# Agent attention and two feed-forward layers: nine query blocks' probabilities turned by VectorE and transfers while the layers run, query scores as two column tiles, and a new order of the opening

## The chip, the cores and the metric

The program runs on one core of a Trainium2 chip. The metric is the device time in microseconds (us) of one execution; the number that counts is the median over executions. A core has TensorE (PE; its weight loads are listed as PEld), VectorE (DVE), ScalarE (ACT), GpSimd (POOL) and SyncE (SP), which here issues nearly all transfers. Inputs and output lie in HBM; the engines work on SBUF and PSUM.

## The reference

```python
# q, k, v: [1, 12480, 128]; agents: [1, 49, 128]; all float32
a2k = softmax(scale * agents @ k.T)          # [49, 12480]
agent_v = a2k @ v                            # [49, 128]
q2a = softmax(scale * q @ agents.T)          # [12480, 49]
x = q2a @ agent_v                            # [12480, 128]
h = x @ w_in;   x = (h * sigmoid(h)) @ w_out # w_in [128, 2048], w_out [2048, 128], float64
h = x @ w2_in;  out = (h * cos(h)) @ w2_out  # the second layer, of the same sizes
```

## The kernel before

**Opening.** The 12480 tokens are cut into 13 blocks S: twelve of 1024 tokens (128 partitions by 8) and one of 192. For each block of k: `kT` turns it on PE (8 transposes), `kX` copies the turned block out of PSUM on ACT, `kS` makes the 49 agents' scores on PE, `kM` keeps them and their maximum on DVE. After the last k block the maximum is known (`x0` to `x4`); then `vE` (ACT), `vt` (PE), `vc` (ACT), `va` (PE) sum the probabilities times v. For each block of q: `qT` and `qX` turn it, `qS` makes the scores (PE, line 379), `qM`, `qB`, `qE`, `qZ`, `qR` make the softmax on DVE and ACT, `qN` scales it on POOL. Then `qP`, `qK`, `qL` on POOL pack high part, low part and a part of the high one again into 128 rows, `qt` turns the pack on PE in two halves of 4 transposes (line 440), and `qk` copies each half out of PSUM into the tile `pT` on ACT (line 445). `pT` is what the first layer multiplies, token by token; `qt` and `qk` of all 13 blocks stand in the opening or among the first groups.

The weights come as float64 in 16 pieces, each split by integer and float operations into a high and a low float32 part: `dA` and `dH` on ACT, `d0` to `d4` and `dL` on DVE. At the end of the opening `c0` to `c6`, `cA`, `cP`, `cl`, `cH`, `cs` and `cw` multiply the attention's sums into the first layer's weights, so that the first layer reads probabilities in place of x. Of 98 rows the product's high and low parts fit 128 partitions but for 19, which a second, small product adds (line 689) from the tile `x`, loaded out of `pT` by four transfers.

**Order.** Every engine works through its own instructions in the order in which they are written. Three hand-written tables set it: `ORDER` (the opening), `FIRST` (the first layer's groups 0 to 4 with what is left of the opening) and `LOADS` (the transfers of weight pieces w, and blocks k, q, v). A load waits until a buffer is free: 5 for k and q together, 3 for w, 3 for v. SP issues them in the table's order.

**Layers.** Tokens go in 25 tiles t of 512 (the last three are shorter); each tile has four groups, so there are 100 groups g. From group 5 on a loop body does the first layer's group g and, beside it, the second layer's group q = g - 5: per group 40 matmuls of 512 columns and four small ones on PE. Of the other engines' work the prediction uses these: ACT line 789 (rounds h / 2 pi) releases DVE line 799 (the remainder), ACT line 808 (sine), DVE line 816 (times h; one operand in PSUM), DVE line 825 (cast to the high part), POOL line 834 (low part, two per group, started after DVE line 724). DVE line 724 is the first layer's low part (both operands in SBUF). PE's three pairs of PSUM banks go round: the second layer's `L2_h(q, 0)` (line 775) takes the pair that DVE line 816 of the group before has freed. `L2_end` (line 856) turns a finished tile 32 by 32 on DVE and SP stores it.

Of the kernel before, what the change touches and what calls it, by code (L numbers as in the profile page):

```python
# [39 lines left out]
kX10 qR0 dL3 qN0 dA5 kM8 kT9 qM1 qP0 qB1 kS10 qK0 qL0 qE1 qT2 kX9 qZ1 d05 qt0.0 qX2 d15 kT11 qR1 d34 qk0.0 qN1  # L40
kS9 dA6 kM10 kT12 d44 kX11 qS2 qP1 kM9 dH5 qK1 d25 qL1 qt0.1 qM2 kS11 qk0.1 qB2 kX12 qt1.0 d35 qE2 qT3 qk1.0 d06
dL4 kS12 qX3 qT4 kM11 d45 dA7 qt1.1 qS3 d16 qX4 d07 kM12 dH6 x0 qZ2 qT5 qk1.1 d17 x1 qR2 qS4 dH7 qM3 qN2 qX5 x2
qP2 qB3 qK2 x3 qT6 qE3 x4 qL2 qM4 vE12 qZ3 qS5 vE0 d26 qR3 dL5 qN3 qX6 qt2.0 qB4 qT7 d27 qE4 qP3 dA8 qZ4 vt1 qK3
qT8 qM5 qk2.0 qL3 qB5 qX7 qt2.1 qR4 d08 qS6 qN4 qk2.1 d36 vc1 qP4 qE5 vt0 vE2 qM6 qT9 qK4 qB6 qL4 qZ5 qt3.0 vc0
d46 va1 qX8 d18 vt3 qk3.0 vt2 d28 vc3 qR5 va0 d37 qN5 vc2 dL6 qE6 qt3.1 va3 qk3.1 qP5 vE4 d47 qT10 qK5 qt4.0 dA9
qZ6 vt4 qL5 dH8 d09 qS7 qk4.0 d38 vc4 dL7 vE8 qt5.0 qS8 qR6 d19 qN6 qk5.0 qM7 dA10 qB7 qt4.1 qX9 d29 vt5 d48 qP6
va2 qk4.1 qM8 qE7 qK6 qB8 va4 qL6 vE6 qZ7 qt5.1 d39 qS9 vc5 dL8 vE10 qR7 d010 qN7 vt6 qM9 qE8 va5 qB9 qP7 vc6 z0
qK7 d110 vt7 dA11 qL7 va6 qk5.1 qZ8 vc7 z1 qt6.0 qX10 z2 d210 vt9 d310 qT11 qk6.0 d011 dH9 d111 qt6.1 qE9 qS10
qR8 d49 qk6.1 qN8 qZ9 dH11 qR9 vc9 qT12 dL9 qP8 qt7.0 dH10 va7 qM10 qX11 qK8 d410 vt10 qN9 qk7.0 va9 qB10 dL10
qE10 qt7.1 qX12 qS11 dA12 qP9 qZ10 qL8 z3 vc10 d012 qk7.1 qK9 vt8 dA13 qM11 qt8.0 qL9 vc8 va10 qB11 qk8.0 d013  # L50
# [897 lines left out]
```

## Time and profile before

| | |
|---|---|
| median of 3 executions | 1080.2 us (1079.47 to 1080.25) |
| span of the profiled execution, first to last instruction | 1076.8 us |
| own time of the profiled execution | not listed apart; 1080.2 less 1076.8 leaves 3.4 us around the span |
| PE busy | 1065.2 us (99%) |
| DVE busy | 964.1 us (90%) |
| ACT busy | 909.8 us (84%) |
| POOL busy | 504.0 us (47%) |
| granted TensorE clock, mean | 0.999 |

A busy PE is not PE at its peak: matmuls overlap, their ends are modelled, and what counts is the distance from one start to the next. Idle time of an engine costs something only where another waits for it.

### The profile page before, as it was taken

The page shows a single profiled execution, that of the slowest core. Times are in us where ns is not written, and L with a number is a line of the kernel's source. Part 1 is how long each engine was busy: PE and PEld are TensorE (multiplying, and loading weights), DVE is VectorE, ACT ScalarE, POOL GpSimd, SP SyncE. Part 2 cuts the span into 40 slices and gives each one's busy share as a digit, 9 for nine tenths or more (in the row PEclk, how much of TensorE's full clock was granted, in tenths as well). Part 3 has the DMA queues.
Part 4 walks back from the last instruction along what each step waited for, and adds up shares of the span by engine and source line. Part 5 has one row for each costly group of instructions (what it writes and reads, how often), then busy time and mean ns, then how long its engine had stood idle before and what let it go on. Part 6 is the DMA issues. An engine that isn't in the chain of part 4 may idle for free.

```text
span 1076.8 us, 14174 instructions
## 1 busy us (share of the span) xinstructions
PE 1065.2 (99%) x5267; PEld 841.2 (78%) x5267; DVE 964.1 (90%) x1067; ACT 909.8 (84%) x972; POOL 504.0 (47%) x264
## 2 busy tenths in 40 slices
PE   9999999999999999999999999999999999999997
PEld 5897777777777777777777777777777777788996
DVE  7877999989999999999989998999999999999897
ACT  5888988888888888888888888888888888888876
POOL 0445044554455445544554455445544554455555
PEclk9999999999999999999999999999999999999999
DMA  9963000000000000000000000000000000000000
GB/s 345 344 226 125 9 6 11 6 16 13 4 16 16 1 17 16 1 16 17 10 6 16 12 5 16 13 4 16 17 1 16 16 1 15 15 11 5 12 9 15
DMA packets 66221, 38.68 MB, mean 36 GB/s; under 512 B 52523, under 2 KB 57184, under 8 KB 66152
## 3 DMA queue, kind: packets, MB, share of 16 engines
q1 hardware_dynamic: 65352, 37.68, 11.5%
q8 instruction: 41, 0.67, 0.3%
q14 instruction: 28, 0.23, 0.1%
q10 hardware_dynamic: 800, 0.10, 0.1%
HBM read 27.58 MB, written 6.39 MB: 32 GB/s over the span
## 4 chain that ended last, share of the span: by engine, by line
PE 95%; DVE 2%; ACT 1%; POOL 1%; DMA 1%; issue 1%; SPq 0%; POOLq 0%; DVEq 0%; ACTq 0%
PE y L733 16%; PE y L737 16%; PE y L734 16%; PE h L701 10%; PE h L775 8%; PE h L777 8%; PE h L776 8%; PE h L689 4%; PE h L267 2%; PE h L379 2%; PE h L303 1%; PE y L366 1%; PE y L440 1%; POOL g2l L834 1%; DMA kraw<-in_k_dram 1%; DVE g L816 1%
## 5 line engine op out<-in xcount | busy, mean ns | idle before, releaser
L834 POOL TENSOR_TENSOR g2l<-g,g2h 128x1024 fp32r<-128x1024 f32 (+2 forms) x200 | 465.5, 2349 | 498.7 <-DVE g1l L724 489.0
L799 DVE SCALAR_TENSOR_TENSOR n<-n,h 128x1024 f32<-128x1024 int32 (+3 forms) x202 | 239.0, 1184 | 63.9 <-ACT n L789 50.8
L789 ACT ACTIVATE n<-h,quarter 128x1024 int32<-128x1024 f32 (+3 forms) x202 | 219.8, 1088 | 88.7 <-PE h L777 88.6
L724 DVE TENSOR_TENSOR g1l<-g,g1h 128x1024 fp32r<-128x1024 f32 (+2 forms) x200 | 239.7, 1199 | 9.7 <-ACT g1h L716 4.1
L816 DVE TENSOR_TENSOR g<-n,h 128x1024 f32<-128x1024 f32 (+3 forms) x202 | 238.0, 1179 | 4.0 <-ACT n L808 0.7
L709 ACT ACTIVATE g<-h 128x1024 f32<-128x1024 f32 (+2 forms) x200 | 199.4, 997 | 36.2 <-PE h L701 36.0
L808 ACT ACTIVATE n<-n,halfpi 128x1024 f32<-128x1024 f32 (+3 forms) x202 | 225.6, 1119 | 0.8 <-DVE n L799 0.8
L716 ACT CAST g1h<-g 128x1024 fp32r<-128x1024 f32 (+2 forms) x200 | 204.9, 1025 | 3.2
L825 DVE CAST g2h<-g 128x1024 fp32r<-128x1024 f32 (+2 forms) x196 | 155.5, 794 | 7.5
L733 PE MATMUL y<-g1h,o1h 128*128 128x512 f32 (+2 forms) x400 | 156.4, 391 | 0.1
L733 PE MATMUL y<-g2h,o2h 128*128 128x512 f32 (+2 forms) x400 | 154.9, 387 | 1.1 <-DVE o L856 0.9
L775 PE MATMUL h<-x2h,i2h 128*128 128x512 f32 (+2 forms) x400 | 154.2, 386 | 1.0 <-DVE g L816 1.0
L734 PE MATMUL y<-g2h,o2l 128*128 128x512 f32 (+2 forms) x400 | 154.5, 386 | 0.0
L734 PE MATMUL y<-g1h,o1l 128*128 128x512 f32 (+2 forms) x400 | 154.0, 385 | 0.0
L777 PE MATMUL h<-x2l,i2h 128*128 128x512 f32 (+2 forms) x400 | 153.9, 385 | 0.0
L776 PE MATMUL h<-x2h,i2l 128*128 128x512 f32 (+2 forms) x400 | 153.9, 385 | 0.0
L701 PE MATMUL h<-pT,w2h 128*128 128x512 f32 (+2 forms) x400 | 132.3, 413 | 0.0
L737 PE MATMUL y<-g2l,o2h 128*128 128x512 f32 (+2 forms) x400 | 122.3, 387 | 1.9 <-POOL g2l L834 1.9
L737 PE MATMUL y<-g1l,o1h 128*128 128x512 f32 (+2 forms) x400 | 121.2, 384 | 0.0
L733 PEld LDWEIGHTS y<-g1h,o1h 128*128 128x128 f32 x400 | 75.1, 188 | 21.1 <-DVE x2l L762 7.8
L701 PEld LDWEIGHTS h<-pT,w2h 128*128 128x128 f32 x400 | 67.3, 188 | 30.9 <-issue 23.9
L737 PEld LDWEIGHTS y<-g2l,o2h 128*128 128x128 f32 x400 | 74.9, 188 | 17.7 <-POOL g2l L834 3.1
(140 smaller groups left out, 1092.5 us busy)
## 6 DMA issues: line engine op xcount, KB each, us to landing
qraw<-in_q_dram SPq DMA_DIRECT2D x12, 512.0 KB
vraw<-in_v_dram SPq DMA_DIRECT2D x12, 512.0 KB
kraw<-in_k_dram SPq DMA_DIRECT2D x11, 512.0 KB
out_dram<-o SPq DMA_DIRECT2D x88, 64.0 KB
wraw<-in_moe_w_in_dram SPq DMA_DIRECT2D x8, 512.0 KB
wraw<-in_moe_w_out_dram SPq DMA_DIRECT2D x8, 512.0 KB
x<-pT SPq DMA_DIRECT2D x88, 38.0 KB
kraw<-in_k_dram SPq DMA_DIRECT2D x2, 256.0 KB
```

Source lines behind the costliest of these rows:

```text
L701: nc.tensor.matmul(out=h1s[g, k][:, j, :toks(t)], lhsT=w2h[:, 128 * c:128 * c + 128], rhs=x, start=False, stop=True)
L724: i = v.tensor_tensor(out=gl, in0=f, in1=b32(gh), op=ALU.subtract)
L733: nc.tensor.matmul(out=y, lhsT=wh[:, c, :], rhs=gh[:, j, :], start=(c == 0), stop=False)
L734: nc.tensor.matmul(out=y, lhsT=wl[:, c, :], rhs=gh[:, j, :], start=False, stop=False)
L737: nc.tensor.matmul(out=y, lhsT=wh[:, c, :], rhs=gl[:, j, :], start=False, stop=(c == NCH - 1))
L775: nc.tensor.matmul(out=y, lhsT=i2h[:, c, :], rhs=xh, start=True, stop=False)
L776: nc.tensor.matmul(out=y, lhsT=i2l[:, c, :], rhs=xh, start=False, stop=False)
L777: nc.tensor.matmul(out=y, lhsT=i2h[:, c, :], rhs=xl, start=False, stop=True)
L799: v.scalar_tensor_tensor(out=b32(n)[:, p], in0=n[:, p], scalar=-2.0 * PI, in1=h2s[g, k][:, p], op0=ALU.mult, op1=ALU.add)
L808: sc.activation(out=r[:, p], in_=r[:, p], func=AF.Sin, bias=halfpi)
L816: v.tensor_tensor(out=f[:, p], in0=r[:, p], in1=h[:, p], op=ALU.mult)
L834: i = (v if (g, k) == (NG - 1, 1) else gp).tensor_tensor(out=gl[:, p], in0=f[:, p], in1=b32(gh)[:, p], op=ALU.subtract)
```

## The change

Of blocks 2 to 10 (`LATE`) `qP`, `qK`, `qL`, `qt` and `qk` leave the opening: `qN` writes the softmax into a stash in SBUF, and while the layers run `P_hi` and `P_lo` on POOL pack half a block (one tile of 512 tokens) at a time, `P_turn` turns the pack on DVE in blocks of 32 by 32, SP writes it to a scratch tensor in HBM and reads it back with four transfers into `pT`. That is done two tiles ahead, for tiles 4 to 21 (18 times). The tokens of these blocks are loaded by four transfers of 32 partitions each in place of one of 128, and their output is stored in the matching order. `qS` uses two column tiles of 64 by 49 for each matmul of 128 by 98. The three tables are new; fillers `wy` are gone from `FIRST`. The tables' lines say little by themselves, so one of each stands here.

```diff
+LATE = (2, 3, 4, 5, 6, 7, 8, 9, 10)
+HOME = {2: 8, 3: 9, 4: 10, 5: 0, 6: 1, 7: 2, 8: 3, 9: 4, 10: 0}
+STASH = {2: (2, 0), 5: (2, 1), 3: (3, 0), 6: (3, 1), 4: (4, 0), 7: (4, 1), 8: (5, 0), 9: (5, 1), 10: (6, 0)}
+STAGE = 7
...
-dA0 d00 d10 kT0 wm3 d20 dH0 d30 kX0 d40 kT1 dL0 kS0 kX1 kT2 kM0 dA1 kS1 kX2 d01 d11 kT3 kM1 dH1 kS2 d21 kX3 d31
+dA3 d03 d13 dA1 d23 dH3 d01 kT8 d11 d33 dH1 qT0 kX8 d41 d43 qX0 kS8 dL3 d21 kT4 kM8 dA2 d31 qS0 kX4 d02 kT11 d12 qM0
...
-w0 k0 k1 k2 w1 k3 k4 k5 w2 q0 k6 w3 k7 k8 w4 q1 k10 w5 k9 q2 k12 k11 w6 v1 q3 v0 q4 w7 q5 q10 q6 w8 q8 q7 v3 q9
+w3 w1 k8 q0 k4 w2 k11 k0 k5 k2 w4 k3 k7 q1 w0 q3 k10 k9 k1 v0 w5 v3 q4 k12 w6 k6 v1 q2 w7 q6 w8 q8 q11 q5 q10 q9 q7 w9
...
+            if key == "q" and S in LATE:
+                src = q[0, blocks[S][0]:blocks[S][0] + 1024, :].rearrange("(x i a s) c -> a i x (s c)", x=2, i=32, s=4)
+                for a in range(4):
+                    nc.sync.dma_start(
+                        out=t[32 * a:32 * a + 32].rearrange("i (x s) c -> i x (s c)", x=2), in_=src[a]
+                    )
+                return t
...
             for i in range(n):
-                nc.tensor.matmul(
-                    out=ps[:p, NA * i:NA * i + 2 * NA], lhsT=xt[:, i // h, p * (i % h):p * (i % h) + p], rhs=ag2,
-                    start=True, stop=True,
-                )
+                for x in range(0, p, 64):
+                    w = min(64, p - x)
+                    at = p * (i % h) + x
+                    nc.tensor.matmul(
+                        out=ps[x:x + w, NA * i:NA * i + NA], lhsT=xt[:, i // h, at:at + w], rhs=agT,
+                        start=True, stop=True, tile_position=(0, x),
+                    )
...
+        def P_hi(t, after_op):
+            if not half(t):
+                return
+            e, pk = late_in(t)
+            i = gp.tensor_copy(out=pk[:, :, 0:NA], in_=e)
+            tc.add_manual_dep(i.ins, after_op.ins.name, AFTER, reason="one at a time on the port to SBUF")
+            gp.tensor_copy(out=pk[:, :, 2 * NA:128], in_=e[:, :, 0:MORE])
...
+            i = gp.tensor_tensor(out=pk[:, :, NA:2 * NA], in0=e, in1=b32(pk)[:, :, 0:NA], op=ALU.subtract)
...
+            v.transpose(
+                out=b32(stage(1)).rearrange("p (x s i) -> p s x i", x=4, i=32),
+                in_=b32(stage(0)).rearrange("p (s x i) -> p s x i", x=4, i=32),
+            )
+            d = scratch.tile([128, 4, 128], F32, tag="turned", name="turned")
+            nc.sync.dma_start(out=d, in_=b32(stage(1)).rearrange("p (x c) -> p x c", x=4))
+            for x in range(4):
+                nc.sync.dma_start(
+                    out=b32(pT(WIDE * t, WIDE))[32 * x:32 * x + 32, :].rearrange("j (a c) -> j a c", a=4),
+                    in_=d[:, x, :].rearrange("(a j) c -> j a c", j=32),
                 )
...
-            L2_hi(q - 1, 0)
+            hi = L2_hi(q - 1, 0)
             L1_h(g, 0)
+            if g % 4 == 0:
+                P_hi(g // 4 + 2, hi)
+            if g % 4 == 1:
+                P_lo(g // 4 + 2, hi)
...
             L2_n(q, 1)
+            if g % 4 == 3:
+                P_turn(g // 4 + 2)
             L2_r(q, 0)
```

Three places show what the tables and the new calls do to the engines. First, PE late in the opening before: L267 turns q, L440 turns packed probabilities, L379 makes scores, L346 and L366 are the v part.

```order
L440 MATMUL y_1108<-ident,pk 128x128 x4
L346 MATMUL h_1117<-ident,sT 128x128 x4
L267 MATMUL h_1125<-ident,qraw 128x128 x8
L440 MATMUL y_1139<-ident,pk 128x128 x4
L379 MATMUL h_1145<-agT,xT 128x98 x8
L267 MATMUL h_1164<-ident,qraw 128x96 x2
L440 MATMUL y_1170<-ident,pk 128x128 x4
L366 MATMUL y_194<-vraw,eT 49x128 x8
```

The same part of the opening on PE in the change (L287 turns q, L401 makes scores, L366 and L386 are the v part):

```order
L287 MATMUL h_1142<-ident,qraw 128x96 x2
L366 MATMUL h_1146<-ident,sT 128x128 x4
L386 MATMUL y_197<-vraw,eT 49x128 x8
L366 MATMUL h_1171<-ident,sT 128x128 x4
L366 MATMUL h_1177<-ident,sT 128x128 x4
L366 MATMUL h_1190<-ident,sT 96x128
L386 MATMUL y_197<-vraw,eT 49x128 x16
L401 MATMUL h_1220<-agT,xT 64x49 x16
```

The turns of packs are gone from between scores and sums, and a block's 8 score matmuls are 16 of half the width and half the columns.

Second, DVE around a `P_turn` in the layers of the change (L821 was L799, L838 was L816, L847 was L825, L746 was L724):

```order
L838 TENSOR_TENSOR g_3574<-n,h_3504 128x1024
L746 TENSOR_TENSOR g1l<-g_3538,g1h 128x1024
L847 CAST g2h<-g_3574 128x1024
L746 TENSOR_TENSOR g1l<-g_3576,g1h 128x1024
L911 STREAM_TRANSPOSE stage<-stage 128x4x4x32
L821 SCALAR_TENSOR_TENSOR n<-n,h_3580 128x1024
L821 SCALAR_TENSOR_TENSOR n<-n,h 128x1024
```

The new transpose stands between the second low part and the first remainder; before, the remainder followed the low part directly.

Third, POOL in the layers of the change, where before there was nothing but L834 (here L857):

```order
L857 TENSOR_TENSOR g2l<-g_3574,g2h 128x1024
L897 CAST stage<-stash 128x4x49
L899 CAST stage<-stash 128x4x30
L857 TENSOR_TENSOR g2l<-g_3635,g2h 128x1024
L857 TENSOR_TENSOR g2l<-g_3664,g2h 128x1024
L905 TENSOR_TENSOR stage<-stash,stage 128x4x49
L857 TENSOR_TENSOR g2l<-g_3721,g2h 128x1024
```

Once in four groups two copies, and one group later a subtraction, stand between one pair of low parts and the next.

## Rows read from the trace of the kernel before

**Rows 1.** The page's first part: span, and busy time by engine.
```profile
span 1076.8 us, 14174 instructions
PE 1065.2 (99%) x5267; PEld 841.2 (78%) x5267; DVE 964.1 (90%) x1067; ACT 909.8 (84%) x972; POOL 504.0 (47%) x264
```
**Rows 2.** Busy time of each engine in stretches, us from the span's start.
```profile
core 0: us, PE busy (x) PEld busy (x) DVE busy (x) ACT busy (x) POOL busy (x), PEclk, DMA share, GB/s
10.00:50.00 40.00, 40.00 (x287) 27.84 (x286) 33.34 (x79) 29.42 (x41) 8.89 (x12) 1.00 1.02 382
50.00:102.00 52.00, 51.75 (x526) 46.65 (x525) 41.30 (x89) 43.89 (x83) 25.50 (x37) 1.00 0.56 193
102.00:128.37 26.37, 25.08 (x128) 18.25 (x128) 24.94 (x37) 25.88 (x32) 3.12 (x6) 1.00 0.04 14
...
165.00:400.00 235.00, 235.00 (x1058) 182.61 (x1057) 213.94 (x205) 201.80 (x199) 114.83 (x48) 1.00 0.05 11
```
**Rows 3.** PE in order of time late in the opening: start, duration, instruction, count.
```profile
79.85 0.60 PE L440 MATMUL y<-ident,pk 128*128 128x128 f32 x4
80.29 1.93 PE L379 MATMUL h<-agT,xT 128*128 128x98 f32 x16
82.05 0.33 PE L267 MATMUL h<-ident,qraw 96*128 96x96 f32 x2
...
92.69 1.30 PE L366 MATMUL y<-vraw,eT 128*49 128x128 f32 x20
...
101.99 0.50 PE L689 MATMUL h<-x,w 19*128 19x512 f32 x3
```
**Rows 4.** Weight loads of PE up to 102 us, by line: busy, mean ns.
```profile
L379 PEld LDWEIGHTS h<-agT,xT 128*128 128x128 f32 (+1 forms) x196 | 22.8, 192 | 0.2 <-issue 0.2
...
L366 PEld LDWEIGHTS y<-vraw,eT 128*49 128x49 f32 (+1 forms) x196 | 10.2, 124 | 1.9 <-issue 1.9
```
**Rows 5.** Line 303, one block: duration min/median/max, first and last start.
```profile
L303 PEld LDWEIGHTS h<-xT,agk x4: 133/134/136, 20.6 to 20.7; 128*64 128x64 f32 x4
L303 PE MATMUL h<-xT,agk x4: 592/618/644, 20.6 to 21.1; 128*64 128x512 f32 x4
```
**Rows 6.** PE in order of time, the same block and its successor.
```profile
20.62 1.08 PE L303 MATMUL h<-xT,agk 128*64 128x512 f32 x4
21.63 1.09 PE L267 MATMUL h<-ident,kraw 128*128 128x128 f32 x8
```
**Rows 7.** Who waited for whom, 10 to 102 us: total, times, longest.
```profile
DVE m L388 <- PE h L379: 6.2, 6, 1.8
...
DVE sT L308 <- PE h L303: 1.5, 3, 0.6
```
**Rows 8.** Groups by line, the whole span: ACT, POOL and DVE work that moves.
```profile
L856 DVE STREAM_TRANSPOSE o<-y 128x512 f32<-128x512 f32 (+2 forms) x25 | 17.4, 696 | 0.7 <-PE y L737 0.7
L445 ACT CAST pT<-y 128x512 fp32r<-128x512 f32 (+1 forms) x25 | 14.4, 577 | 4.2 <-PE y L440 4.0
...
L429 POOL TENSOR_TENSOR pk<-e,pk 128x392 fp32r<-128x392 f32 (+1 forms) x13 | 12.0, 924 | 0.0
...
L422 POOL CAST pk<-e 128x392 fp32r<-128x392 f32 (+1 forms) x13 | 7.9, 607 | 5.6 <-PE y L440 4.5 <-PE h L346 0.5
```
**Rows 9.** DVE in order of time, one group of the layers.
```profile
407.63 1.15 DVE L825 CAST g2h<-g 128x1024 fp32r<-128x1024 f32 x1
408.70 1.21 DVE L816 TENSOR_TENSOR g<-n,h 128x1024 f32<-128x1024 f32 x1
409.83 1.22 DVE L724 TENSOR_TENSOR g1l<-g,g1h 128x1024 fp32r<-128x1024 f32 x1
410.96 0.68 DVE L825 CAST g2h<-g 128x1024 fp32r<-128x1024 f32 x1
411.78 1.23 DVE L724 TENSOR_TENSOR g1l<-g,g1h 128x1024 fp32r<-128x1024 f32 x1
413.52 1.22 DVE L799 SCALAR_TENSOR_TENSOR n<-n,h 128x1024 f32<-128x1024 int32 x1 [0.52 <-ACT n L789]
```
**Rows 10.** POOL in order of time, the same group.
```profile
403.44 4.78 POOL L834 TENSOR_TENSOR g2l<-g,g2h 128x1024 fp32r<-128x1024 f32 x2 [5.03 <-DVE g1l L724]
413.17 4.78 POOL L834 TENSOR_TENSOR g2l<-g,g2h 128x1024 fp32r<-128x1024 f32 x2 [4.95 <-DVE g1l L724]
```
**Rows 11.** PE in order of time, the same group: the second layer's first matmul.
```profile
410.81 0.39 PE L775 MATMUL h<-x2h,i2h 128*128 128x512 f32 x1
```
**Rows 12.** SP in order of time: one issue of a q block's load.
```profile
10.56 0.39 SPq L210 DMA_DIRECT2D qraw<-in_q_dram  x1
```

More of the change, by code (lines that the diff above doesn't have):

```diff
@@ L40 @@
[L40 to L44, printed above, removed]
@@ L100, in agent_attention_moe_moe_kernel @@
     halfpi = const.tile([128, 1], F32, name="halfpi")
-    const.tile([128, LINE - 8], F32, name="fill")
+    const.tile([128, LINE + 40], F32, name="fill")
     turned = {}
@@ L247, in agent_attention_moe_moe_kernel @@
         nc.vector.tensor_copy(out=agk[:, 0:NA], in_=pa[:, :NA])
-        for j in range(2):
-            nc.vector.tensor_copy(out=agT[:, j, :], in_=pa[:, :NA])
+        nc.vector.tensor_copy(out=agT, in_=pa[:, :NA])
         for x in (0, 64):
@@ L281, in wy, with turned_copy @@
             unit(banky("y2")[:, 0:128], n)
-        def turned_copy(key, S):
+        def turned_copy(key, S, copy=nc.scalar.copy):
             pt = had.pop(("pt", key, S))
             xt = xT_p.tile([128, 2, 512], F32, tag="xT", name="xT")[:, :, :pt.shape[2]]
-            nc.scalar.copy(out=xt, in_=pt)
+            copy(out=xt, in_=pt)
             had["xT", key, S] = xt
@@ L347, in vt, with vc @@
             had["vt", S] = pe[:p, :64 * n].rearrange("p (s a) -> p s a", a=128)
-        def vc(S):
+        def vc(S, copy=nc.scalar.copy):
             _, p, n = blocks[S]
             eT = had["eT", S] = eT_p.tile([128, 4, 128], F32, tag="eT", name="eT")[:p, :n // 2]
-            nc.scalar.copy(out=eT, in_=had.pop(("vt", S)))
+            copy(out=eT, in_=had.pop(("vt", S)))
         sums = banky("y1")
@@ L471, in d1, with dH, d2 @@
             )
-        def dH(S):
+        def dH(S, copy=nc.scalar.copy):
             hi, lo = dest(S)
-            nc.scalar.copy(out=hi, in_=had["da", S][0].bitcast(F32))
-        def d2(S):
+            copy(out=hi, in_=had["da", S][0].bitcast(F32))
+        def d2(S, eng=nc.vector):
             a, m = had["da", S]
-            nc.vector.tensor_scalar(
+            eng.tensor_scalar(
                 out=m.bitcast(U32), in0=a, scalar1=0xFF800000, scalar2=None, op0=ALU.bitwise_and
@@ L710, in L1_act, with L1_hi @@
             g1s[g, k] = [f]
-        def L1_hi(g, k):
+        def L1_hi(g, k, copy=nc.scalar.copy):
             if not 0 <= g < NG:
@@ L715, in L1_hi @@
             gh = wide(g1h_p, "g1h", F32R, g)
-            sc.copy(out=gh, in_=g1s[g, k][0])
+            copy(out=gh, in_=g1s[g, k][0])
             g1s[g, k].append(gh)
@@ L824, in L2_hi @@
             for p in parts(g):
-                (sc.copy if k and g + LAG >= NG else v.tensor_copy)(out=gh[:, p], in_=g2s[g, k][0][:, p])
+                i = (sc.copy if k and g + LAG >= NG else v.tensor_copy)(out=gh[:, p], in_=g2s[g, k][0][:, p])
             g2s[g, k].append(gh)
+            return i
         def L2_lo(g, k):
```

79 lines of the change are left out of this document (52 added, 27 removed).

## The prediction

> **What bounds the kernel now.** I read the page first, then the busy times by stretch, then the waits of the opening, and last the order in time of one group in the layers. PE is busy 99% of the span [rows 1], and from 165 us on it has no gap at all: 235.00 of 235.00 us [rows 2]. The layers' time is therefore the sum of PE's own matmuls, and the change takes none of them away. Time can come only from what lies ahead: the opening up to the first product of the first layer, which starts at 101.99 us [rows 3], and the first groups, up to 128.4 us. From 10 to 102 us PE is again busy throughout (91.75 of 92 us), DVE 74.64 (33.34 and 41.30), ACT 73.31, and the transfers 40 x 1.02 + 52 x 0.56 = 69.9 [rows 2]. So PE sets the opening's pace, with DVE as the next bound 17.4 us below it. From 102 to 128.4 us ACT is busy 25.88 of 26.37 us and DVE 24.94 [rows 2]: there PE waits for them, and PE work saved in that stretch is worth nothing.
>
> **What leaves PE in the opening.** Four turns of a pack take 0.44 us, from 79.85 to 80.29 [rows 3]. The nine late blocks have 18 such groups; 17 of them stood ahead of the first layer, so 17 x 0.44 = 7.5 us go there. The eighteenth stood among the first groups and gives nothing.
>
> **The scores.** A block's 16 rows take 1.76 us, 80.29 to 82.05 [rows 3], or 110 ns a row. A load of 128 columns lasts 192 ns and one of 49 lasts 124 [rows 4]: 68 ns for 79 columns, 0.86 ns a column, and 128 x 0.86 = 110. The pace is thus set by the loads, not by the 98 moving columns. A half-width load needs 64 x 0.86 = 55 ns, but there are 32 rows now. If the two column tiles load and multiply side by side, a block takes 16 x 55 = 0.88 us; if one after the other, 32 x 55 = 1.76 us, as before. Column tiles of 64 are in the trace already: line 303 has two halves with two rows each. All four loads start between 20.6 and 20.7 us and none is longer than 136 ns, and the matmuls start at 20.6 and 21.1 [rows 5]; all four are over in 1.01 us, 20.62 to 21.63 [rows 6], two steps of 0.5, not four. So the halves run together. For going in and out of the tiling I choose an allowance of 0.1 us a block and take 0.98 us: 12 x (1.76 - 0.98) = 9.4 us saved. The other end, tiles one after the other with the same 0.1, is 1.2 us lost. Below 0.98 I see no row.
>
> **What of it shows.** PE saves 7.5 + 9.4 = 16.9 us and would need about 75 of the 92 us. DVE keeps its instructions (one copy of the agents less) and its 74.64. So both are at about 75, and neither can fill the time alone, since each waits for the other in turn. Of DVE's 17.4 idle us, waits for the two kinds of scores are 6.2 + 1.5 = 7.7 [rows 7]; these shrink when PE runs ahead. The others are chains (the maximum, the sums) that the change does not shorten. The lower end is therefore 7.7 and the upper 16.9, if the new order fills the chains as well. I take 9, near the lower end, because DVE, the engine that now has least room, loses no work. Of the others: ACT loses 17 copies of 0.577 us [rows 8], 9.8 us, and is not the bound. [...] SP issues 27 transfers more for the late q blocks, at 0.39 us each [rows 12] 10.5 us over the opening, hidden as long as buffers are what SP waits for.
>
> **What the layers take on.** 18 times a tile's work is added beside four groups of 9.73 us (403.44 to 413.17 [rows 10]). The turn on DVE: the like turn out of PSUM takes 0.70 us [rows 8]; I take the same from SBUF, between 0.5 and 1.4. It stands where DVE waits 0.52 us for ACT [rows 9], so the remainder starts 0.18 us late (0.70 - 0.52). What is late next is the product of line 816, and then PE's line 775, which needs its PSUM pair: the product ends at 408.70 + 1.21 = 409.91, the matmul starts at 410.81 [rows 9, 11], a slack of 0.90 us. Even 1.4 us would stay within it, so the cost is 0. POOL is free 4.95 us in each group [rows 10]. Its two copies have 196 and 120 columns against the 392 that take 0.607 us [rows 8], together under that; the subtraction has half the columns of one that takes 0.924. They start after the cast that ends at 408.78 and run beside a product with an operand in PSUM; the next DVE instruction with both operands in SBUF starts at 409.83 [rows 9]. About 1.05 us are there, so the cost is 0. That POOL and DVE do hold one another up shows in the first cast: 1.15 us against 0.68 for the second [rows 9], and POOL's pair ends at 403.44 + 4.78 = 408.22 [rows 10]. On SP the reads of the scratch tensor wait until the store has landed, and behind them stand the 19-row loads, issued two groups later, and the next stores; 19 us lie between, and the transfers are at a share of 0.05 [rows 2]. Cost 0; without that cover, PE would wait for its first layer's input, some us at each tile.
>
> **Sum.** The span of 1076.8 us less 9 is 1067.8; with the 3.4 us around it 1071.2, against the median of 1080.2.
>
> **Rivals.**
> *The loads become the bound.* A late q block now comes in four transfers onto 32 partitions each. No row shows the rate of such a load. At 382 GB/s [rows 2] 512 KB take 1.37 us; at half that, nine blocks take 12.3 us more, and the transfers need 69.9 + 12.3 = 82.2 us after 10 us; from the last v product to the first layer it is 9.3 us more (92.69 to 101.99 [rows 3]). That gives 101.5 if no transfer waits, a gain of nearly nothing; since a part of those transfers lies in that tail, I put the gain at 2: 1078.2 us. It decides from about 4 us of added transfer time. For it speaks that transfers are saturated to 50 us; against it that from 50 to 102 us they are used to 0.56. [...]
> *The column tiles do not overlap.* PE then needs 91.75 - 7.5 + 1.2 = 85.5 us, and DVE keeps most of its 6.2 us of waiting for scores. The gain is about 4: 1076.2 us. Rows 5 speak against it.
> *Slower: the turn on DVE is held by POOL.* POOL's low parts start 0.16 us after the low part on DVE ends (413.17 against 411.78 + 1.23 [rows 9, 10]), so turn and subtraction start nearly together. If the turn had to wait for the first subtraction (half of 4.78, 2.4 us), the remainder would be 2.4 + 0.70 - 0.52 = 2.6 us late, 1.7 beyond the slack, 18 times 31 us: 1102 us. It decides from 0.5 us a tile beyond the slack (9 / 18). Against it: the turn needs no second operand, and DVE reaches it first.
> *The change frees PE, and the opening does not get shorter,* as the first k block is now third in the loads and buffers or chains take over: 1079.5 us.
> *More than expected:* the new order fills the chains too, gain 15: 1065 us.
>
> **Chances and range.** Forecast 0.58, more 0.10, loads 0.12, tiles 0.10, slower 0.06, no shorter opening 0.04. The forecast alone holds 1067.5 to 1074.5 (gains of 6 to 13). To leave out no more than 2 in 10, the range goes from 1064.5, which takes in most of the larger gain, to 1078.2, which takes in the tiles and half of the loads. A measurement can tell about 0.2%, 2.2 us, from no change: faster means below 1078.0, slower above 1082.4. Faster: 0.58 + 0.10 + 0.10 + half of 0.12 = 0.84. Same: 0.06 + 0.04 = 0.10. Slower 0.06.
>
> **What the profile will show.** Right: the first 19-row product starts near 93 us in place of 101.99, and 128.4 becomes 119.5; a block's 32 score rows take about 1.0 us; DVE's wait for scores falls from 6.2 to some 1 to 2 us and DVE is busy 85% or more; from there to the end PE has no gaps, and a turn of 0.6 to 0.7 us lies in DVE's wait for ACT. Wrong: score blocks of 1.8 us; a share of transfers near 1 beyond 60 us with PE and DVE waiting for q or v; gaps of PE at line 775 once in four groups; a first stretch that is shorter by less than 5 us while 102 to 128 grows by what it saved.

## The result and the profile after

The change made the kernel slower: 1088.6 us median (1087.8 to 1091.2, 4 runs) against 1079.8 for the kernel before (1078.9 to 1080.3), a ratio of 1.0091 with a 95% interval of 1.0076 to 1.0106. The profiled execution took 1088.43 us, its span is 1086.7 us.

The page's first parts, of the changed kernel (they answer to [rows 1]):

```profile
span 1086.7 us, 14620 instructions
...
PE 1058.8 (97%) x5375; PEld 830.6 (76%) x5375; DVE 974.5 (90%) x1084; ACT 900.9 (83%) x954; POOL 508.8 (47%) x291
...
PEclk9988899999999999999999999999999999999998
DMA  9975000110110010011011011001001100000000
GB/s 330 302 231 166 10 7 1 35 31 10 31 34 12 26 36 20 16 36 30 7 36 32 9 30 36 11 26 35 22 15 35 30 6 16 15 11 5 10 9 16
```

PE is no longer busy 99% of the span, and the row of its granted clock has eights in the third to fifth slice. The busy times by stretch of the changed kernel, cut where the granted clock changes (they answer to [rows 2]):

```profile
core 0: us, PE busy (x) PEld busy (x) DVE busy (x) ACT busy (x) POOL busy (x), PEclk, DMA share, GB/s
...
10.00:56.40 46.40, 40.62 (x402) 27.91 (x402) 37.43 (x84) 30.35 (x42) 7.90 (x9) 0.98 1.05 322
56.40:63.20 6.80, 5.54 (x46) 5.21 (x42) 4.96 (x10) 3.88 (x6) 0.84 (x1) 0.50 0.78 218
63.20:97.40 34.20, 29.19 (x473) 25.08 (x471) 28.67 (x63) 25.53 (x48) 8.23 (x10) 1.00 0.70 236
97.40:104.20 6.80, 5.62 (x25) 5.27 (x24) 3.41 (x7) 3.08 (x9) 1.12 (x4) 0.50 0.27 87
104.20:111.00 6.80, 5.43 (x26) 3.45 (x25) 5.58 (x12) 4.33 (x8) 0.00 (x0) 1.00 0.07 28
111.00:117.80 6.80, 6.42 (x19) 4.07 (x18) 6.21 (x9) 6.67 (x8) 0.00 (x0) 0.50 0.03 10
117.80:135.60 17.80, 17.33 (x82) 12.49 (x82) 15.22 (x21) 15.89 (x20) 3.58 (x4) 1.00 0.03 9
...
145.10:148.60 3.50, 3.50 (x10) 2.69 (x9) 2.87 (x4) 2.02 (x2) 1.19 (x1) 0.51 0.00 0
165.00:1000.00 835.00, 834.90 (x3769) 650.92 (x3768) 768.56 (x747) 716.44 (x708) 430.17 (x224) 1.00 0.09 23
...
1080.40:1086.70 6.30, 2.09 (x7) 1.58 (x6) 1.12 (x3) 0.00 (x0) 0.00 (x0) 0.50 0.19 31
```

Three things are to be seen. From 10 to 56.4 us the transfers' share is 1.05, they are saturated, yet they move 322 GB/s; before, a share of 1.02 moved 382 [rows 2]. PE is busy 40.62 of those 46.4 us, where it had no gap before. And there are stretches with the granted clock at 0.50 in the opening, the first groups, at the loop's start and at the end; before, it fell to 0.50 only in the last 1.1 us (from 1075.7 us).

Who waited for whom, 0 to 136 us of the changed kernel: total, times, longest. None of these four rows was there before in this size (before, such waits came to 3.0 us in all for `w_in` and to less for any other load):

```profile
ACT m L481 <- DMA wraw<-in_moe_w_out_dram: 6.0, 4, 2.7
...
ACT m L481 <- DMA wraw<-in_moe_w_in_dram: 5.2, 3, 2.6
...
PE y L386 <- DMA vraw<-in_v_dram: 2.7, 3, 1.2
PE h L287 <- DMA qraw<-in_q_dram: 2.6, 3, 1.3
```

PE in order of time at the end of the opening of the changed kernel (start, duration, and in brackets the wait before; answers to [rows 3]):

```profile
93.04 1.08 PE L386 MATMUL y<-vraw,eT 128*49 128x128 f32 x16 [0.92 <-DMA vraw<-in_v_dram]
94.05 0.38 PE L527 MATMUL h<-rz,both 128*128 128x1 f32 x2
94.94 0.43 PE L386 MATMUL y<-vraw,eT 96*49 96x128 f32 x4 [0.51 <-DMA vraw<-in_v_dram]
96.95 0.51 PE L552 MATMUL h<-eye,halves 128*128 128x160 f32 x2 [1.58 <-DVE z L433]
98.64 0.58 PE L462 MATMUL y<-ident,pk 96*128 96x96 f32 x2 [1.18 <-POOL pk L451]
...
107.08 0.50 PE L711 MATMUL h<-x,w 19*128 19x512 f32 x3
```

The last v blocks come late, two waits of a chain follow, and the first 19-row product starts at 107.08 us in place of 101.99.

The following table takes the span apart at four starts on PE: the first 19-row product, the loop's first second-layer matmul, that of its third group, and that of its hundredth (line 797, before line 775). Its rows are differences of starts in the two traces.

| us | before | after | difference |
|---|---|---|---|
| up to the first 19-row product | 101.99 | 107.08 | +5.1 |
| first groups, from there to the loop | 26.38 | 28.52 | +2.1 |
| the loop's first two groups | 17.91 | 19.37 | +1.5 |
| third to hundredth group | 916.23 | 916.27 | 0.0 |
| from there to the end | 14.33 | 15.43 | +1.1 |

So the change's work in the layers costs nothing, and all of the 9.8 us lie where the order, the loads and the clock changed. (The two profiled spans differ by 9.8 us, the medians by 8.8.)

### The profile page after: what moved, and what is told of

The parts are those of the page before. It is cut to its first block, busy times and chain, and to the rows that moved or that the text cites. A ratio compares the mean times of both kernels' runs of the same rounds, so it can differ in the third digit from the quotient of the medians.

```text
span 1086.7 us, 14620 instructions
## 1 busy us (share of the span) xinstructions
PE 1058.8 (97%) x5375; PEld 830.6 (76%) x5375; DVE 974.5 (90%) x1084; ACT 900.9 (83%) x954; POOL 508.8 (47%) x291
## 4 chain that ended last, share of the span: by engine, by line
PE 91%; DMA 4%; ACT 2%; DVE 1%; POOL 0%; SPq 0%; issue 0%; POOLq 0%; ACTq 0%; DVEq 0%
PE y L755 16%; PE y L759 16%; PE y L756 16%; PE h L723 10%; PE h L797 8%; PE h L799 8%; PE h L798 8%; PE h L711 4%; DMA qraw<-in_q_dram 2%; PE h L287 2%; PE h L323 1%; DMA x<-pT 1%; DMA kraw<-in_k_dram 1%; DMA wraw<-in_moe_w_in_dram 1%; PE y L386 1%; DMA vraw<-in_v_dram 1%
## 5 line engine op out<-in xcount | busy, mean ns | idle before, releaser
L857 POOL TENSOR_TENSOR g2l<-g,g2h 128x1024 fp32r<-128x1024 f32 (+2 forms) x200 | 465.5, 2349 | 434.8 <-DVE g1l L746 425.0
L821 DVE SCALAR_TENSOR_TENSOR n<-n,h 128x1024 f32<-128x1024 int32 (+3 forms) x202 | 238.9, 1184 | 55.7 <-ACT n L811 42.9
L746 DVE TENSOR_TENSOR g1l<-g,g1h 128x1024 fp32r<-128x1024 f32 (+2 forms) x200 | 240.3, 1202 | 12.8 <-ACT g1h L738 7.1
L838 DVE TENSOR_TENSOR g<-n,h 128x1024 f32<-128x1024 f32 (+3 forms) x202 | 238.0, 1179 | 4.2 <-issue 0.8
L738 ACT CAST g1h<-g 128x1024 fp32r<-128x1024 f32 (+2 forms) x200 | 204.9, 1024 | 3.3
L847 DVE CAST g2h<-g 128x1024 fp32r<-128x1024 f32 (+2 forms) x196 | 152.9, 781 | 7.9 <-DVE g L838 0.5
L799 PE MATMUL h<-x2l,i2h 128*128 128x512 f32 (+2 forms) x400 | 154.3, 386 | 0.0
```

Of the source, the lines that this page charges most:

```text
L746: i = v.tensor_tensor(out=gl, in0=f, in1=b32(gh), op=ALU.subtract)
L799: nc.tensor.matmul(out=y, lhsT=i2h[:, c, :], rhs=xl, start=False, stop=True)
L821: v.scalar_tensor_tensor(out=b32(n)[:, p], in0=n[:, p], scalar=-2.0 * PI, in1=h2s[g, k][:, p], op0=ALU.mult, op1=ALU.add)
L838: v.tensor_tensor(out=f[:, p], in0=r[:, p], in1=h[:, p], op=ALU.mult)
L857: i = (v if (g, k) == (NG - 1, 1) else gp).tensor_tensor(out=gl[:, p], in0=f[:, p], in1=b32(gh)[:, p], op=ALU.subtract)
```

## Experiments

All kernels are the changed kernel or the one before with the edit shown. Times are medians; ratios are to the kernel before on the same chip (1078.5 to 1078.9 us), with 95% intervals. The last columns are from each profile: the first 19-row product, the first groups, the loop's first two groups, the stretch from the hundredth group to the end, all in us. Each of these columns is one execution: the kernels with column tiles alone and with 2 transfers of 128 are 0.2 us apart in time and 1.35 in the first product, so a difference of that size in one column is no effect by itself.

| kernel | time | ratio | first product | first groups | two groups | end |
|---|---|---|---|---|---|---|
| wide loads | 1079.1 | 1.0002 (0.9990 to 1.0015) | 97.96 | 28.20 | 18.37 | 15.58 |
| fillers | 1091.8 | 1.0119 (1.0097 to 1.0142) | 111.54 | 28.76 | 19.34 | 14.51 |
| wide loads, fillers | 1088.1 | 1.0088 (1.0066 to 1.0110) | 107.14 | 28.19 | 19.40 | 15.60 |
| column tiles alone | 1074.6 | 0.9960 (0.9948 to 0.9972) | 98.02 | 26.38 | 17.91 | 14.36 |
| old tables, wide loads | 1072.5 | 0.9940 (0.9925 to 0.9955) | 96.17 | 27.70 | 17.92 | 14.50 |
| wide, few fillers | 1080.7 | 1.0019 (1.0007 to 1.0030) | 96.61 | 31.52 | 18.34 | 14.52 |
| 4 transfers of 32 | 1090.0 | 1.0099 (1.0078 to 1.0120) | 110.08 | 26.38 | 17.93 | 14.59 |
| 4 transfers of 128 | 1079.7 | 1.0002 (0.9991 to 1.0012) | 101.59 | 27.89 | 17.93 | 14.57 |
| old tables, wide, fillers | 1072.4 | 0.9937 (0.9920 to 0.9953) | 94.51 | 27.87 | 19.02 | 14.52 |
| old tables, 32 partitions | 1086.9 | 1.0073 (1.0058 to 1.0088) | 109.15 | 27.86 | 17.92 | 14.56 |
| wide, fillers at the tail | 1079.7 | 1.0004 (0.9994 to 1.0015) | 97.52 | 29.71 | 19.34 | 15.60 |
| wide, k first | 1078.3 | 0.9994 (0.9984 to 1.0004) | 98.13 | 28.29 | 19.41 | 15.62 |
| 2 transfers of 128 | 1074.8 | 0.9960 (0.9950 to 0.9971) | 96.67 | 27.92 | 17.94 | 14.43 |
| 2 transfers of 64 | 1090.6 | 1.0107 (1.0089 to 1.0124) | 113.91 | 27.86 | 17.91 | 14.45 |
| wide, tail reordered | 1079.5 | 1.0003 (0.9994 to 1.0013) | 98.47 | 28.60 | 19.41 | 15.63 |

**The loads undone** (wide loads). The turn's order of tokens is made in `qX`'s copy in place of the load:

```diff
-            if key == "q" and S in LATE:
-                src = q[...].rearrange("(x i a s) c -> a i x (s c)", x=2, i=32, s=4)
-                for a in range(4):
-                    nc.sync.dma_start(out=t[32 * a:32 * a + 32]..., in_=src[a])
-                return t
...
+            if key == "q" and S in LATE:
+                copy(
+                    out=xt.rearrange("c x (s a i) -> c (x s) a i", a=4, i=32),
+                    in_=pt.rearrange("c x (s i a) -> c (x s) a i", a=4, i=32),
+                )
+            else:
+                copy(out=xt, in_=pt)
```

> The change with the nine late q blocks loaded by one transfer onto 128 partitions, as before; the order of tokens that the change's turn wants is made by the copy out of PSUM instead (same columns, read with a stride of four). Loads theory (four transfers of 32 partitions each took the transfers' time): the mean 2 KB packet between 51 and 60 us, 128 ns in the change, goes back to about 85 ns, the nine blocks need about 6 us less, the waits for q, k, v and the weight pieces shrink, and the first 19-row product comes at about 100 us in place of 107.1; time about 1081 us. [...] Order theory (the three tables make the opening longer by their chains): packets get shorter but the first product stays at 105 us or later, about 1087 us.

Measured: 1079.1 us, 9.5 less than the change, and the first product at 97.96. ACT's copies with the stride take 1017 ns on average and those without 1012, so the new order of tokens is free this way. This is the loads theory, with a little more given back than its 1081 us and 100; but the time is that of the kernel before and no gain is left, and half-clock stretches remain (from 8.2, 86.7 and 100.4 us, and at the end; the granted clock was 0.50 from 86.7 to 93.5 us).

**Fillers everywhere.** `wm` and `wy` steps of 3 to 18 matmuls, whose result nobody uses, ahead of twelve steps of the order, without and with the wide loads. They try the clock theory, by which the stretches at a granted clock of 0.50 cost the time:

```diff
+ wm18 kT8 ... wm12 kT6 ... wm4 qT4 ... wm8 qt1.1 ... wm8 x1 ... wm4 qT8 ... wy8 qT5
+ ... wy8 va4 ... wy6 va11 ... wy3 va12 ... wy10 c2 ... wy8 qt12.0
```

> The change with matmuls of no use (128 x 128, some 0.13 us each, 3 to 18 of them) put into PE's order at the twelve places where PE waited 0.4 to 2.4 us in the opening. Clock theory: the granted clock stays at 1.0 up to 118 us, which gives back about 2.6 us of 97.4 to 104.2, up to 3 of 111.0 to 117.8 and 1.4 of 145.1 to 148.6; time about 1082 us. Loads theory: up to 97 us PE waits for transfers at either clock, so the fillers give back only what lies behind, 2.6 us at most; 1086 us or more. Fillers that delay work of use would show as a first 19-row product behind 107.1 us.

> Both edits together, loads onto 128 partitions and the fillers. If loads and clock each cost and their costs add, about 1088.6 less 7 less 6, near 1076 us, below the kernel before. If only the loads cost, the same as the first edit alone, near 1081; if only the clock, near 1082; if the order's own chains cost, above 1085.

Measured: 1091.8 and 1088.1 us, both worse than without. The expectations' length of a filler was wrong. PE in order of time, in the run with both edits, the first 18 (two records each):

```profile
5.20 4.29 PE L289 MATMUL y<-ident 128*128 128x128 f32 x36
```

That is 0.24 us each and 4.29 in all, in a wait of 2.41 us in the change and of 2.97 with wide loads: the k block behind it starts at 9.32 in place of 8.44 us. The clock stayed at 1.0 up to 110 us in that run, but the work of use came later by more than that gave: the first product at 107.1 in place of 97.96. As a test of the clock this pair decides nothing; it shows that what these fillers were longer than their waits was paid.

**One part alone.** The kernel before with the scores' column tiles:

```diff
-                nc.tensor.matmul(
-                    out=ps[:p, NA * i:NA * i + 2 * NA], lhsT=xt[:, i // h, p * (i % h):p * (i % h) + p], rhs=ag2,
+                for x in range(0, p, 64):
...
+                        out=ps[x:x + w, NA * i:NA * i + NA], lhsT=xt[:, i // h, at:at + w], rhs=agT[:, 0, :],
+                        start=True, stop=True, tile_position=(0, x),
```

> The kernel before with one part of the change: the q scores as two column tiles of 64 by 49, everything else as before (old tables, turns of packs on PE, loads onto 128 partitions). By the prediction a block's scores take 0.98 us in place of 1.76, PE gets 9.4 us and about 4 of them show, since DVE is next with 17 us of room in 92: about 1076 us. [...]

Measured: 1074.6 us, the first product 4.0 us earlier, nothing else changed and no half-clock stretch before the last microsecond (the granted clock was 1.00 up to 124.4 us). The prediction's view held for this part: 4.3 us gained (from 1078.9) where about 4 were expected.

**The change in the old order.** Wide loads, column tiles and late turns, but the old tables without the nine blocks' `qP`, `qK`, `qL`, `qt`, `qk`:

```diff
-dA3 d03 d13 dA1 d23 dH3 d01 kT8 d11 d33 dH1 qT0 kX8 ...
+dA0 d00 d10 kT0 wm3 d20 dH0 d30 kX0 d40 kT1 dL0 kS0 ...
```

> The whole change but for two parts: loads onto 128 partitions (as in the run before), and the old three tables, from which only the steps of blocks 2 to 10 that pack, turn and copy (qP, qK, qL, qt, qk) are dropped. Beside the run of column tiles alone it tells what the turns bring when they leave the opening in the old order. Prediction's view (PE sets the pace): 17 turns of 0.44 us leave, the first 19-row product comes at about 94 us in place of 98.0, time about 1071 us. Order theory (the new tables, not the turn, cost what the wide loads did not give back, 4.5 us between 1079.1 and 1074.6): at most 1074.6 us, first layer and first groups as in the kernel before, 26.4 us from the first 19-row product to the loop. Clock theory: with PE's fillers and turns gone from the opening, half-clock stretches come here too, and the time is 1076 us or more.

Measured: 1072.5 us, faster than both kernels. Against column tiles alone the first product is 1.85 us earlier and the time 2.1 less (the intervals of the two ratios still overlap, 0.9925 to 0.9955 and 0.9948 to 0.9972), with half-clock stretches at 51.1, 75.0 and 98.9 us (the mean granted clock was 0.79 from 51.2 to 59.0 us and from 75.2 to 83.0); with these the first groups take 27.7 in place of 26.4 us. So each theory is right in a part (the stretches came, but not the clock theory's 1076 us), and the new tables cost 6.6 us beside wide loads (1079.1 against 1072.5).

**Few fillers** (wide, few fillers; then wide, fillers at the tail).

```diff
+ ... wy2 va11 ... wy4 va12 ... wy8 c2 ... wy3 qt12.0      (opening)
+ ... LR1 cH3 wy8 Lh1.0                                     (first groups; left out in the second run)
```

> The change with loads onto 128 partitions, and with few fillers, shorter than the waits they stand in: 2, 4, 8 and 3 matmuls at the last sums and the chain behind them, and 8 in the first groups where the kernel before had 8. Clock theory: the half-clock stretches from 86.7 and from 100.4 us go away, about 1.4 us in the products of the weights with the attention's sums and 1.8 in the first groups are given back, time about 1076 us. Order theory (waits of the new order's chain, not the clock): the stretches move or go and the time stays within 1 us of 1079.1.

> The change with wide loads (1079.1 us) and the few fillers at the last sums and the chain behind them, without the 8 in the first groups. With those the first 19-row product came at 96.6 in place of 98.0 us, but the first groups grew to 31.5 us. Clock theory: 96.6 stays, the first groups take 28.2 us as without fillers, time about 1077.7. If the 8 were not what lengthened the first groups: 31 us again and 1080 or more.

Measured: 1080.7 and 1079.7 us. With both groups the first product came at 96.6, as the clock theory said, and the first groups grew to 31.5 us; without those eight they took 29.7, not 28.2. The clock fell in the first groups in both (from 100.8 and 101.8 us), as it does without any filler (100.4). New in both is a wait of PE for DVE between the first 19-row products; it accounts for 1.1 of the 1.5 us between 29.7 and 28.2. In the second run:

```profile
97.52 0.94 PE L710 MATMUL h<-x,w 19*128 19x512 f32 x2
99.58 0.47 PE L710 MATMUL h<-x,w 19*128 19x512 f32 x1 [1.12 <-DVE halfpi L674]
```

Nothing is gained in the end by either.

**The disputed load by itself.** In the kernel with column tiles alone, tokens where they were, the nine blocks' loads cut in four, first by partitions (4 transfers of 32), then by tokens (4 transfers of 128):

```diff
+            if key == "q" and 2 <= S <= 10:
+                for a in range(4):
+                    nc.sync.dma_start(out=dst[32 * a:32 * a + 32], in_=src[32 * a:32 * a + 32])
+                return t
...
+                for x in range(2):
+                    for y in range(2):
+                        nc.sync.dma_start(out=dst[:, x, 2 * y:2 * y + 2, :], in_=src[:, x, 2 * y:2 * y + 2, :])
```

> The disputed cost by itself: the kernel before with column tiles (1074.6 us), in which the q blocks 2 to 10 are loaded by four transfers of 32 partitions each, with tokens where they were and the same packets of 2 KB. Theory of the partitions: 2 KB packets take about 128 ns in place of 85, the nine blocks need about 6 us more transfer time, and the opening grows by 2 to 6 us: 1077 to 1080 us. Rival (the slow packets in the change come from the order of its loads, or from tokens 32 KB apart in HBM): packets stay near 85 ns and the time near 1074.6.

> The counter-check to the run before it: the same nine blocks in four transfers each, but each onto all 128 partitions, two tokens of 512 B per partition, so packets of 1 KB. If it is the partitions that count, 1 KB packets take the 49 ns that the weight pieces' do in the kernel before, and the time stays within 1.5 us of 1074.6. If it is the number of transfers (27 issues more on SP, 0.39 us each), packets or issues get slow here too and the time is as in the run before it.

Measured: 1090.0 and 1079.7 us. Thirty-two partitions cost 15.4 us, over twice what was expected at most, in an order in which nothing else changed. The counter-check cost 5.1, more than the 1.5 expected, though its packets were not slow (49 and 89 ns, in the table below); so it did not settle whether the number of transfers counts. Two more kernels differ in partitions alone, both with two transfers per block and packets of 2 KB, first 2 transfers of 128, then 2 of 64:

```diff
+                for x in range(2):
+                    nc.sync.dma_start(out=dst[:, x], in_=src[:, x])
...
+                for a in range(2):
+                    nc.sync.dma_start(out=dst[64 * a:64 * a + 64], in_=src[64 * a:64 * a + 64])
```

> Column tiles alone (1074.6 us) with the nine q blocks in two transfers each, both onto all 128 partitions, packets of 2 KB as before: the number of transfers alone, 9 issues more. Theory of the partitions: packets stay at 88 ns and the time within 1.5 us of 1074.6. Rival (the number of transfers, through SP's issues of 0.39 us, takes a share of what the split by 32 partitions cost): 9 of its 27 issues, a third of the 5.1 us that four transfers onto 128 partitions cost, about 1076.3 us.

> The same with two transfers of 64 partitions each: as many transfers, as many packets of 2 KB, only half the partitions in each. Theory of the partitions, in proportion: packets between 88 and 129 ns, about 100, and the time some 3 us above the run with two transfers onto 128 partitions. If only the step to 32 partitions matters: 88 ns and the same time as that run.

Measured: 1074.8 and 1090.6 us. Twice as many transfers cost nothing (0.2 us); half the partitions cost 15.8 us, as much as a quarter of them. What of the counter-check's 5.1 us is the number of its transfers and what its smaller packets stays open; beside narrow pieces it does not show, where four cost no more than two. The transfers of the two kernels, 40 to 60 us (GB/s in 40 slices, then the queue's packets, MB and share of the 16 engines' time), first two of 128:

```profile
GB/s 365 371 393 389 389 393 381 389 418 406 397 401 361 377 385 406 401 397 401 385 369 250 176 53 0 0 0 0 139 270 336 254 49 0 0 0 0 213 344 401
...
q1 hardware_dynamic: 2395, 5.28, 72.1%
```

and two of 64:

```profile
GB/s 266 258 213 225 186 227 238 199 240 244 260 221 227 203 229 225 248 223 217 246 234 242 242 234 254 234 225 238 234 254 188 217 229 205 201 246 234 246 275 201
...
q1 hardware_dynamic: 2501, 4.59, 106.1%
```

At full share that is 5.28 MB / (20 us x 0.721) = 366 GB/s against 4.59 / (20 x 1.061) = 216. The mean time of a packet from the same traces' packet records, 12 to 75 us, grouped by size, ns:

| packet | before | column tiles | 2 of 128 | 4 of 128 | 2 of 64 | 4 of 32 | the change | wide loads |
|---|---|---|---|---|---|---|---|---|
| 2 KB (q and others) | 88 | 88 | 88 | 89 | 140 | 129 | 122 | 88 |
| 1 KB (weights; with 4 of 128, q too) | 49 | 49 | 50 | 49 | 59 | 59 | 59 | 50 |

The narrow transfers are slow themselves (122 to 140 ns for a packet of 2 KB in place of 88) and slow down others that run beside them (59 ns for one of 1 KB in place of 49 to 50). In total the same 28.05 MB take the 16 engines 8.3 us longer in the change than with wide loads (130 us x (0.673 - 0.609)). The queue from 0 to 130 us, first the change, then wide loads:

```profile
q1 hardware_dynamic: 13301, 28.05, 67.3%
...
q1 hardware_dynamic: 12872, 28.05, 60.9%
```

**The same loads in the change without its tables.** The kernel with the old tables and late turns, with the change's loads put back:

> The same kernel with the old tables, but with the nine q blocks loaded as the change loads them, four transfers of 32 partitions each; it differs from the change in the tables alone. Loads theory: the loads cost here what they cost beside column tiles alone (15.4 us), near 1088 us, so the change's new tables are not what made it slower. Order theory (the new tables cost 6.5 us beside wide loads and would do so here too): near 1082 us, as the change without them.

Measured: 1086.9 us, 14.4 above the wide loads, as the loads theory said. The four kernels form a square, in us:

| | wide loads | 32 partitions |
|---|---|---|
| old tables | 1072.5 | 1086.9 |
| new tables | 1079.1 | 1088.6 |

(In this kernel packets of 2 KB took 128 ns, those of 1 KB 53.) The loads cost 14.4 in one order and 9.5 in the other; the tables 6.6 with wide loads. The 1.7 with narrow ones is not clear of the noise: the intervals of the two ratios (1.0058 to 1.0088 and 1.0076 to 1.0106) overlap.

**The clock in the best kernel.** Old tables, wide loads, fillers in three waits:

```diff
+ ... wm8 qT7 ... wy4 vt5 ... wy10 va6
```

> The kernel with the old tables, wide loads, column tiles and late turns (1072.5 us), with three groups of fillers in waits of PE for a load or for DVE: 8 matmuls in the wait of 1.89 us at 50.7, 4 in that of 1.09 at 65.8 and 10 in that of 1.96 at 73.9. Clock theory: the half-clock stretches from 51.1 and 75.0 us (8 us each) go away, the last v product and the first 19-row product come 1 to 3 us earlier than 96.2, time about 1070. Rival (in the opening PE waits for loads, DVE and ACT anyway, so its clock costs nothing there): the stretches go, but the first 19-row product stays within 0.7 us of 96.2 and the time within 1 us of 1072.5.

Measured: 1072.4 us, no gain. The busy times by stretch show what happened:

```profile
core 0: us, PE busy (x) PEld busy (x) DVE busy (x) ACT busy (x) POOL busy (x), PEclk, DMA share, GB/s
40.00:94.50 54.50, 51.77 (x715) 45.06 (x713) 46.76 (x107) 41.12 (x76) 10.98 (x13) 1.00 0.71 251
97.00:106.00 9.00, 8.85 (x44) 6.78 (x43) 8.28 (x12) 7.72 (x9) 2.51 (x6) 0.81 0.04 17
131.00:140.00 9.00, 9.00 (x32) 6.59 (x32) 7.25 (x8) 7.03 (x8) 4.76 (x2) 0.81 0.00 0
```

The two stretches in the opening went and the first product came 1.65 us earlier, as the clock theory said; the time stayed, as its rival said. The fall in the first groups was still there, and another came at 131.7 us, where the loop's first two groups took 19.0 in place of 17.9 us. The profiled span is 0.6 us shorter, the median the same.

**Where the new tables lose.** Two edits of the change with wide loads: the first k block first in loads and order; and, in the second, `z4` directly behind `z3` (two steps on DVE behind the last sums of probabilities), with block 12's `qK`, `qL`, `qt`, `qk` moved behind the first layer's start:

```diff
-w3 w1 k8 q0 ...                                  (loads)
+k8 w3 w1 q0 ...
-dA3 d03 d13 dA1 d23 dH3 d01 kT8 ...              (order)
+kT8 kX8 kS8 dA3 d03 d13 dA1 d23 dH3 d01 ...
```

```diff
-... z2 z3 c0 c1 d015 qE12 st qZ12 z4 ... qK12 qL12 c4 c3 c6 qt12.0 ...
+... z2 z3 z4 c0 c1 d015 qE12 st qZ12 ... c4 c3 c6 ...
```

> The change with wide loads, in which the first k block is first among the loads and its turn, copy and scores are first in the order (in the change two weight pieces come first and PE gets its first block at 8.1 to 8.4 us, in the kernel before at 5.7). If the late start costs its full length: the first 19-row product 2.5 us earlier, about 95.5, time about 1076.5. If the opening is set by the transfers' sum, whose order alone changes: within 1 us of 1079.1.

> The change with wide loads (1079.1 us), two pieces of its order moved: z4 directly behind z3 on DVE, and the last small q block's packing and turn (qK, qL, qt, qk of block 12) behind the start of the first layer, as in the kernel before. Order theory: PE's waits of 1.58 us before the product of sums and 0.82 before the turn of that block go, the first 19-row product comes at about 95.6 in place of 98.0 us, time about 1076.7. Clock theory (a wait that goes from one place makes the clock fall at another or lets the half-clock stretch start earlier): the first product comes earlier, but the first groups or the loop's first two groups take it back, time within 1 us of 1079.1.

Measured: 1078.3 and 1079.5 us. With k first PE has its first block at 5.70 us in place of 8.44, and the first product is not earlier: the opening's end is not set by its start. In the other kernel the wait of 1.58 shrank to 0.73, but PE then waited 1.30 us for POOL at the next product, and the first product came at 98.5. Neither names a single wait that holds the new tables back. The three tables (loads, opening, first groups) were not tried one by one, so which of them costs the 6.6 us stays open.

## Why the prediction was wrong

**The step that failed is the cost of the loads.** The forecast's sum gave the late blocks' four transfers no time at all: of 27 more issues it said that they are hidden, and their rate it left to the rival *the loads become the bound*, at a chance of 0.12. That rival was the right one: undoing the loads alone took 9.5 us, as much as the whole loss of 8.8 (the ratio went from 1.0091 to 1.0002). It took the rate for lower than the packets show (a half, an assumption that no run shows; they took 122 to 140 ns in place of 88, a rate of 0.63 to 0.72), but its time was far too small, 1078.2. It worked with the transfers' total after 10 us, 69.9 + 12.3 of 92, and with their share of 0.56 after 50 us as room. The late blocks are loaded between 20 and 63 us, and there the transfers had no room: 1.02 from 10 to 50 us [rows 2]. What is late there is q, v and the weight pieces together, and PE, ACT and DVE wait in turn. The rival's own condition, some 4 us of added transfer time, was met with 8.3.

What the rival had wrong is that the added time would hide beside PE's work until the two sums met: in each of the four pairs of kernels that differ in these loads the time grew by at least as much as the transfers' sum over 130 us, 9.5 us for 8.3 in the change, 14.4 for 10.0 with the old tables, 15.4 for 10.9 and 15.8 for 15.3 with column tiles alone. It should have carried a loss. The sign that the prediction named for it, a share near 1 beyond 60 us, did not come (0.78 from 56.4 us, 0.70 from 63.2); the waits for q and v did.

The number of partitions is all that differs in the pair of 128 and 64 (1074.8 against 1090.6 us), and the cost was not in proportion to it: 15.8 us for two pieces of 64, 15.4 for four of 32. What makes the narrow pieces slow no trace here shows.

**The new tables were given no cost.** The prediction let the new order fill or not fill the chains; it did not ask what it could lose. Beside wide loads it loses 6.6 us. In the profiled runs 3.9 of these are to be found: 1.8 up to the first product, 0.5 in the first groups, 0.45 in the loop's first two groups and 1.1 at the end. The last is the clock, which falls 6 to 7 us before the end in six of the eight profiled kernels with the new tables and in none of the nine with the old ones, where it falls in the last 2 us at most; so it goes with the new tables, though not always, and why is not shown. The other 2.7 us lie between profiled run and median and stay open.

**PE's clock was not in the prediction.** In the kernel before it fell only in the last 1.1 us, behind PE's last matmul. The change takes some 17 us of work from PE and adds waits, and the granted clock drops to 0.50. Where PE sets the pace this costs: from 97.4 to 104.2 us a matmul of 512 columns starts 0.43 us after the last (102.06 to 102.49), later 0.24 (105.61 to 105.85), which over 5.3 us of products is some 2.3 us (5.3 x 0.19 / 0.43); a fall in the first groups costs 1.3 to 1.5 (27.70 to 27.92 against 26.38, six kernels with the old tables against the three with these that kept the clock there, the kernel before among them) and one in the loop's first two groups about 1.0 (19.37 against 18.37, both with the new tables). In the opening it costs up to 1.65, but what the fillers won there did not show in the time. Added up (2.3, 1.4, 1.0, and 1.1 at the end) it is an estimate of some 6 of the 9.8 us. Most of that is not the loads' doing: with the loads undone the stretches in the first groups and at the end are still there at their full price (28.20 and 15.58 us, in the change 28.52 and 15.43), one from 86.7 to 93.5 us still takes in 2.6 us of the weights' products (in the change 5.3), and of the 10.3 us between the two profiled spans (1086.7 and 1076.4) 9.1 lie ahead of the first product. So the clock is rather a part of why the wide loads alone bring no gain. No run changes the clock alone; what makes it fall is not shown.

**The scores were right.** PE in order of time, a block of the changed kernel:

```profile
72.20 1.09 PE L401 MATMUL h<-agT,xT 128*64 128x49 f32 x32
73.22 0.98 PE L287 MATMUL h<-ident,qraw 128*128 128x128 f32 x7
```

32 rows take 1.02 us; predicted was 0.98, and the rival *column tiles do not overlap* needed 1.86. Alone they brought 4.3 us.

**The turns that leave were right, the size too large.** In the old order they brought some 2 us (1074.6 to 1072.5) of the 7.5 that PE saves. The reading that one of the 18 groups of turns stood among the first groups is wrong: all 18 start ahead of 101.99 us, the last at 97.96, but the change moves block 12's turn into the opening, which leaves 7.6 us in place of 7.5 (18 x 0.44 less some 0.3). Both parts together, with wide loads, moved the first product from 101.99 to 96.17, 5.8 us where 9 were taken: the range's low end for the forecast was 6. The 3.4 us that the sum puts around the span hold a second error: in the runs it is 1.7 to 1.8 (1088.43 less 1086.7), and the rest was the distance of the profiled execution from the median. That the forecast's 1071.2 us lies near the 1072.5 of the old order with wide loads is thus in part luck; the gain there is 5.9 us (from 1078.5), not 9.

**The layers were right.** From the third to the hundredth group both kernels take the same time to 0.04 us. The 18 turns on DVE, by line:

```profile
L911 DVE STREAM_TRANSPOSE stage<-stage x18: 703/704/706, 196.2 to 862.1; 128x512 f32<-128x512 f32 x18
```

They take the 0.70 us of the like turn and nobody waits for them; the rival *turn held by POOL* is out. That the turn needs no second operand, which the prediction set against this rival, is not shown to matter: a cast, which has none either, took 1.15 us beside POOL in place of 0.68 [rows 9, 10].

## What to carry to other kernels

Ask of a transfer that is cut first how many partitions each piece has: here two pieces of 128 were free and two of 64 cost 15.8 us of 1074.8. If a layout wants another order of rows, make it in a copy that is there anyway; the strided copy out of PSUM cost nothing here (1017 against 1012 ns). An average share of a resource over a stage is no room for work that falls in the part of the stage where the resource is full (here the transfers' share was 1.02 from 10 to 50 us and 0.56 from there to 102). PE's granted clock fell to 0.50 here in a change that left PE less work and more waits: look in the profile after for the waits that are new, and price a new order for what it may lose too.

## What the runs showed of the hardware beyond what was expected

- Loads onto 64 and onto 32 partitions were about equally slow: from 40 to 60 us a stream with pieces of 64 moved 216 GB/s at full share, one with pieces of 32 (4 transfers of 32) moved 242 (4.60 MB at a share of 0.952), one with 128 moved 366. Packets of 1 KB of other loads beside the narrow ones took 53 to 59 ns (four kernels) in place of 49 to 50.
- PE's granted clock fell to 0.50 in the changed kernel, none of whose waits on PE in the opening was longer than 2.41 us; in the best kernel it fell again further on when waits were filled at one place (51.1 and 75.0 us went, 131.7 came, with a mean of 0.81 from 131 to 140 us). Ahead of the stretches at 56.4 and 97.4 us PE had waited for q (0.62 and 0.75 us) and for v (0.92 and 0.51), but also for ACT (1.21 and 1.14) and DVE (1.58); which of these waits counts is not shown.
- ACT read PSUM at a stride of four columns as fast as in a row: 1017 against 1012 ns for 128 x 1024 (wide loads).
